# Converting float64 weights: rebias, shift, sign and an integer add, 512 columns a piece, and second weights used in place

## The chip, the cores and the metric

The kernel runs on one core of one Trainium2 chip. The time is device microseconds (us) of one execution of the whole program. The engines are TensorE (PE, matrix products; its weight loads are listed apart as PEld), VectorE (DVE), ScalarE (ACT), GpSimd (POOL) and SyncE (SP), which here only issues DMAs. Each engine works through its own instructions in program order; semaphores make it wait for others.

## The reference

The program is an attention followed by a mixing block with a two-layer perceptron, over 8 batches of 576 tokens, 8 heads of 64:

```python
def _attn_ref(q, k, v, s):
    scores = scale * np.matmul(q, k.transpose(0, 1, 3, 2))
    cum = np.cumsum(np.maximum(s, 0.0), axis=-1)
    bias = -(cum[:, :, :, None] - cum[:, :, None, :])
    scores = np.where(causal, -1000000000.0, scores + np.minimum(bias, 0.0))
    ...
    return np.matmul(attn, v)

def _moe_ref(x, w_ch1, w_ch2):
    X = np.fft.fft(np.fft.fft(x, axis=1), axis=2)
    u = x + np.real(X)
    un = (u - mu) / np.sqrt(var + 1e-06)
    ch = np.maximum(un @ w_ch1, 0.0) @ w_ch2
    return u + ch
```

The two weight matrices (512 x 2048 and 2048 x 512) arrive as 64-bit numbers: the host takes numpy's float64 arrays as pairs of 32-bit words and does no arithmetic on them. The kernel makes 32-bit floats of them, 2 million numbers in all. A double's high word has the sign, 11 bits of exponent and the upper 20 bits of the mantissa; the low word has the other 32. A float has 8 bits of exponent and 23 of mantissa.

## The kernel before

**Stages.** The batches' heads are worked off as 32 pairs (stage one, some 545 us): scores, exponentials, products with the values, and the Fourier products of earlier batches woven in. Then comes a transition, in which the attention ends, the last Fourier products run, and the perceptron begins on the first two tiles of 512 tokens. Seven more tiles follow in `fast_tile`.

**Weights.** The 2048 hidden units are 16 groups `f` of 128. For each f, `wP[f]` holds 128 partitions x 1024 numbers: 512 of the first matrix, 512 of the second. The kernel keeps each converted number as a high part (rounded to the matmul's 32-bit format) and a low rest, so that three products give nearly full precision: `wh`, `wl` for the first matrix, `w2h`, `w2l` for the second. The first weights stay in SBUF; the second ones are kept in DRAM (`w2D`) and read again for each tile.

**Conversion.** A piece is WC = 256 columns. Its raw words are loaded (`raw`, 8 bytes a number). `hi` is the high word, `lo` the upper 16 bits of the low word; both are read with a step of 8 bytes. DVE isolates the exponent bits (L85 or L1110); ACT rebiases and scales them (Relu with a bias, L86 or L1112); DVE makes an integer of the mantissa bits (L87 or L1115), adds `lo` scaled by 2^-16 (L90 or L1117), puts the sign onto the exponent's power of two (L89 or L1120); POOL multiplies the two (L91 or L1123).

- For f = 0 to 5 (`NC` = 6) this is done during the attention by `convert_w` (L95), a generator that is woven between the other streams of a pair; its tiles are in the pool `attb`, and the floats go to DRAM (`wD`).
- For f = 6 to 15 (`N1` = 6) it is done in the transition by `piece` (L1099). `late_first` (L1186) makes the first weights, two pieces for each f, split on ACT and DVE by `split_w` (L1127); those of f = 6 and 7 in the pool `stage2`, those of f = 8 to 15 in the pool `stage3`, which opens when the Fourier tables' space is released. `late_second` (L1175) makes the second weights, two pieces for each f, split on ACT and POOL into the buffers `cvh` and `cvl` (two of each); `keep_second` (L1138) stores both to `w2D`.

**Order of the transition.** It is not written out by hand: a small planner (`Flow`, L1613) simulates the engines at build time. Each generator yields steps (engine, cost, what it depends on, a ring of buffers with so many readers) and emits its instruction when the planner picks it: of the steps that can start first on an engine, the one with the earliest due time. Costs come from `act`, `dve`, `dvp`, `pool_` and `dma` (L1678 to L1695). The order in which steps are picked is the order of the instructions on each engine and of the DMAs on SP.

**Steps of the perceptron there.** `todo` (L1310) lists 32 steps n in four parts p: tile one with f = 0 to 5 (p = 0), tile two with f = 0 to 5 (p = 1), tile one with f = 6 to 15 (p = 2, n = 12 to 21), tile two with f = 6 to 15 (p = 3). A step is a first product (L1433: 24 matmuls with `wh`, `wl`), the rectified result split by ACT and DVE (L1299, L1301), and a second product (L1413 to L1415), which PE runs behind the first product of step n + 1. For p > 0, `second_loads` (L1315) reads a step's second weights from `w2D` into one of four slots of the ring `w2`, as soon as the step four before has been multiplied:

```python
            _, hold = yield wait(ev("w2taken"), ring=(ring("w2", 4), 1))
            t = second()
            got = Last(ev("S", n), 2)
            for x in range(2):
                e = yield dma(256, ev("w2D", f))
                nc.sync.dma_start(out=t[x].bitcast(F32), in_=w2D[x, f])
                got.add(e)
            S2[n] = (*t, hold)
```

After the last second weights are stored, `sums_flow` (L1460) forms the sums of first weights that the fast tiles need (`sums_w`, L113).

Of the kernel before, what the change touches and what calls it, by code (L numbers as in the profile page):

```python
# [42 lines left out]
def fused_kernel(ctx, tc, qkT, vA, sP, wP, tabD, tabS, corr, out):  # L43
# [21 lines left out]
    nc.vector.memset(eps, 1e-6)  # L65
    wbias = const.tile([128, 1], F32, name="wbias")
    nc.vector.memset(wbias, -8.0 * WEXP)


# [3 lines left out]

    WC = 256

    def rounded(pool, f, x, bufs):

        m = pool.tile([128, WC], I32, tag="wm", name="wm", bufs=bufs)
        raw = pool.tile([128, 2 * WC], I32, tag="raw", name="raw", bufs=bufs)
        nc.sync.dma_start(out=raw, in_=wP[f, :, WC * x:WC * x + WC].bitcast(I32))  # L80
        hi = raw.rearrange("p (n w) -> p n w", w=2)[:, :, 1]
        lo = raw.bitcast(U16).rearrange("p (n w) -> p n w", w=4)[:, :, 1]
        yield 0.0
        e = pool.tile([128, WC], I32, tag="we", name="we", bufs=bufs)
        nc.vector.tensor_scalar(e, hi, 0x7FF00000, None, op0=ALU.bitwise_and)  # L85
        nc.scalar.activation(e, e, AF.Relu, bias=wbias, scale=8.0)  # L86
        nc.vector.tensor_scalar(m, hi, 0xFFFFF, 0x100000, op0=ALU.bitwise_and, op1=ALU.bitwise_or)  # L87
        yield 0.4
        nc.vector.scalar_tensor_tensor(out=e, in0=hi, scalar=-0x80000000, in1=e, op0=ALU.bitwise_and, op1=ALU.bitwise_or)  # L89
        nc.vector.scalar_tensor_tensor(out=m.bitcast(F32), in0=lo, scalar=2.0 ** -16, in1=m, op0=ALU.mult, op1=ALU.add)  # L90
        nc.gpsimd.tensor_mul(e.bitcast(F32), m.bitcast(F32), e.bitcast(F32))  # L91
        yield 0.4
        return e.bitcast(F32)

    def convert_w(pool, lo, hi, bufs):  # L95

        for f in range(lo, hi):
            for x in range(1024 // WC):
                m = yield from rounded(pool, f, x, bufs)
                nc.sync.dma_start(out=wD[f, :, WC * x:WC * x + WC], in_=m)  # L100
                yield 0.2
# [442 lines left out]
    for M in Ms:  # L544
        nc.vector.memset(M, 0.0)
    amask = att.tile([128, 640], BF16, name="amask")
    nc.gpsimd.memset(amask, 0.0)
    nc.gpsimd.affine_select(out=amask[:, 512:640], in_=amask[:, 512:640], pattern=[[-1, 128]], compare_op=ALU.is_ge, fill=NEG, base=0, channel_multiplier=1)
    trash = att.tile([128, 512], BF16, name="trash")
# [48 lines left out]
    def maxes(i):  # L598
        st = sts[i]
        qy, ky = st["qy"], st["ky"]  # L600
        M = Ms[i % 2]
        M1 = att.tile([128, 4], F32, tag="M1", name="M1", bufs=2)
        for h in range(2):
            for c in range(5):
                nk = 128 * c + 128 if c < 4 else S
                parts = [(0, max(nk, 256))] if c < 4 else [(0, 256), (256, 320)]
                col = M[:, 5 * h + c:5 * h + c + 1]
                for x, (k0, n) in enumerate(parts):
                    p = psm.tile([128, 512], F32, tag="m", name="pm", bufs=5)
                    nc.tensor.matmul(p[:, :n], qy[:, h, 128 * c:128 * c + 128], ky[:, h, k0:k0 + n], start=True, stop=True)  # L610
                    if len(parts) > 1 and not x:
                        first = M1[:, h:h + 1]
                        nc.vector.tensor_reduce(out=first, in_=p[:, :n], axis=AX.X, op=ALU.max)
                    else:
                        n = nk - k0
                        m0 = 512 - 128 * c + k0
                        nc.vector.tensor_tensor_reduce(out=trash[:, :n], in0=p[:, :n], in1=amask[:, m0:m0 + n], scale=1.0,  # L617
                                                       scalar=first if x else NEG, op0=ALU.add, op1=ALU.max, accum_out=col)
# [3 lines left out]
        nc.tensor.transpose(out=p[0:10, 0:128], in_=M, identity=ident)  # L622
# [103 lines left out]
    mixing = None  # L726
    weights = convert_w(attb, 0, NC, 2)
    tiles = list(range(0, NT, TOK))
# [370 lines left out]
    def piece(where, f, x, bufs, then):  # L1099


        e, rhold = yield dma(256, ring=(ring(where + "raw", bufs), 2))
        home = stages[where]
        raw = home.tile([128, 2 * WC], I32, tag="raw", name="raw", bufs=bufs)
        nc.sync.dma_start(out=raw, in_=wP[f, :, WC * x:WC * x + WC].bitcast(I32))
        hi = raw.rearrange("p (n w) -> p n w", w=2)[:, :, 1]
        lo = raw.bitcast(U16).rearrange("p (n w) -> p n w", w=4)[:, :, 1]
        e1, hold = yield ("DVE", 0.42, (e,), (ring(where + "we", bufs), 1))
        n = home.tile([128, WC], I32, tag="we", name="we", bufs=bufs)
        nc.vector.tensor_scalar(n, hi, 0x7FF00000, None, op0=ALU.bitwise_and)  # L1110
        e1 = yield act(400, e1)
        nc.scalar.activation(n, n, AF.Relu, bias=wbias, scale=8.0)  # L1112
        _, mhold = yield ("DVE", 0.42, (e,), (ring(where + "wm", bufs), 1))
        m = home.tile([128, WC], I32, tag="wm", name="wm", bufs=bufs)
        nc.vector.tensor_scalar(m, hi, 0xFFFFF, 0x100000, op0=ALU.bitwise_and, op1=ALU.bitwise_or)  # L1115
        e = yield dve(256)
        nc.vector.scalar_tensor_tensor(out=m.bitcast(F32), in0=lo, scalar=2.0 ** -16, in1=m, op0=ALU.mult, op1=ALU.add)  # L1117
        rhold.add(e)
        e = yield dve(256, e1)
        nc.vector.scalar_tensor_tensor(out=n, in0=hi, scalar=-0x80000000, in1=n, op0=ALU.bitwise_and, op1=ALU.bitwise_or)  # L1120
        rhold.add(e)
        e = yield pool_(256, e)
        nc.gpsimd.tensor_mul(n.bitcast(F32), m.bitcast(F32), n.bitcast(F32))  # L1123
        mhold.add(e)
        yield from then(n.bitcast(F32), e, hold)

# [20 lines left out]
    def load_w(f, home):  # L1147
# [14 lines left out]
        W2now[f] = (vh, vl, hold)  # L1162
        flow.add(keep_second(f, (vh, vl), hold), due_w(f) + 20.0)

# [9 lines left out]

    def late_second():  # L1175


        for f in range(N1, NF):
            _, hold = yield wait(ring=(ring("cv", 2), 2))
            t = [stages["stage2"].tile([128, 512], F32R, tag=f"cv{y}", name=f"cv{y}", bufs=2) for y in "hl"]  # L1180
            ready = Last(ev("W2", f), 2)
            flow.add(keep_second(f, t, hold), late_due(f) - 20.0)
            for x in (2, 3):
                flow.add(piece("stage2", f, x, 4, split_w(*t, slice(WC * x - 512, WC * x - 256), WC, True, ready)), late_due(f) - 30.0 + x)

    def late_first(home, where, bufs, f0, f1):  # L1186
        for f in range(f0, f1):
            wh = home.tile([128, 512], F32R, tag=f"wh{f}", name=f"wh{f}")
            wl = home.tile([128, 512], F32R, tag=f"wl{f}", name=f"wl{f}")
            W[f] = (wh, wl)  # L1190
            ready = Last(ev("W", f), 2)
            for x in (0, 1):
                flow.add(piece(where, f, x, bufs, split_w(wh, wl, slice(WC * x, WC * x + WC), WC, False, ready)), late_due(f) - 20.0 + x)

# [272 lines left out]
    def tail():  # L1467
# [222 lines left out]
def pool_(n, *deps, ring=None):  # L1690
    return "POOL", 0.15 + n * 0.0024, deps, ring

# [157 lines left out]
```

## Time and profile before

| | us |
|---|---|
| three runs | 1436.44, 1430.39, 1432.87 |
| median | 1432.87 |
| the profiled execution, its own time | 1428.06 |
| its span, first to last instruction | 1426.3 |
| stage 0 to 545 (attention) | 545 |
| stage 545 to 814 (transition) | 269 |
| stage 814 to 1426 (fast tiles) | 612 |

The mean granted clock of TensorE in that execution is 0.967 of full speed. In the profile, L12 is line 12 of the kernel's source; `out<-in` names the tiles written and read; a group's row gives the count, the busy time in us and the mean duration in ns, and then how long the engine had stood idle before these instructions and for whom. In a row by tile, the three durations are the smallest, the median and the largest in ns. Matmuls are pipelined, so a busy PE isn't PE at its peak.

### The profile page before, as it was taken

How to read it: one execution, taken by the hardware profiler on the slowest of the kernel's cores; microseconds unless marked ns; L12 is line 12 of the kernel's file. 1: busy time of each engine (PE TensorE's matmuls, PEld its weight loads, DVE VectorE, ACT ScalarE, POOL GpSimd, SP SyncE). 2: the span in 40 equal slices, each digit the busy share in tenths (PEclk: the TensorE clock that was granted, in tenths of full speed). 3: DMA queues.
4: the chain of work that ended last, by engine and by line, in shares of the span. 5: the costliest groups of instructions: out<-in, count | busy, mean ns of one | idle time of the engine just before them, and what ended most of it. 6: DMA issues, size and time to landing. Idle time of an engine off the chain costs nothing.

```text
span 1426.3 us, 21949 instructions
## 1 busy us (share of the span) xinstructions
PE 1285.1 (90%) x7582; PEld 1122.4 (79%) x7582; DVE 878.1 (62%) x1989; ACT 627.8 (44%) x1472; POOL 522.1 (37%) x541
## 2 busy tenths in 40 slices
PE   4886979797979898889879989999999999999998
PEld 3665867686867677779768878888888888898987
DVE  6667686768685756798984477544445453544423
ACT  4664757474756565543432333333333333333221
POOL 6444565556564646545562243110201111021100
PEclk9999999898999999999979999999999999999999
DMA  8565555464655545648644332534434343343333
GB/s 198 155 186 157 144 163 159 149 168 152 170 161 145 153 117 162 211 152 279 226 162 158 111 118 89 170 126 142 144 121 161 103 159 129 128 157 104 134 119 118
DMA packets 128907, 216.06 MB, mean 151 GB/s; under 512 B 16826, under 2 KB 41850, under 8 KB 128796
## 3 DMA queue, kind: packets, MB, share of 16 engines
q1 hardware_dynamic: 126795, 211.60, 48.5%
q0 software_dynamic: 1712, 2.53, 0.9%
q8 instruction: 60, 0.98, 0.3%
q10 hardware_dynamic: 288, 0.52, 0.1%
q14 instruction: 52, 0.42, 0.1%
HBM read 158.93 MB, written 31.72 MB: 134 GB/s over the span
## 4 chain that ended last, share of the span: by engine, by line
PE 48%; DVE 8%; POOL 2%; issue 1%; ACT 1%; DMA 1%; SPq 0%; POOLq 0%; DVEq 0%; ACTq 0%
PE b L331 19%; PE acc L242 7%; PE acc L243 7%; PE acc L244 7%; PE h L1433 3%; PE acc L1415 1%; PE acc L1414 1%; PE acc L1413 1%; DVE wm L1117 1%; DVE we L1120 1%; DVE we L1110 1%; DVE wm L1115 1%; DVE wl L1132 1%; PE pz L1005 1%; DVE zl L1301 1%
## 5 line engine op out<-in xcount | busy, mean ns | idle before, releaser
L610 PE MATMUL pm<-KQ 128*128 128x256 f32 (+3 forms) x384 | 157.7, 430 | 46.4 <-DVE Mx L617 26.7
L646 ACT ACTIVATE P<-ps 128x256 f32<-128x256 f32 x372 | 141.7, 393 | 121.6 <-PE ps L643 117.6
L674 PE MATMUL pavB<-P,va 128*128 128x320 f32 x600 | 180.8, 394 | 9.4 <-ACT stage L678 9.4
L242 PE MATMUL acc<-zh,w2h 128*128 128x512 f32 x452 | 179.0, 396 | 0.0
L243 PE MATMUL acc<-zh,w2l 128*128 128x512 f32 x452 | 179.0, 396 | 0.0
L244 PE MATMUL acc<-zl,w2h 128*128 128x512 f32 x452 | 178.4, 395 | 0.0
L289 POOL TENSOR_TENSOR w<-w,o 128x512 f32<-128x512 f32 x28 | 37.9, 1364 | 353.4 <-DVE o L285 312.8
L642 PE MATMUL ps<-KQ 128*128 128x256 f32 x372 | 148.7, 403 | 14.6 <-ACT P L646 5.8
L617 DVE CUSTOM_DVE_ANT_0 trash<-pm,amask 128x128 bf16<-128x128 f32 (+3 forms) x256 | 123.6, 483 | 42.8 <-PE pm L610 25.8
L610 PEld LDWEIGHTS pm<-KQ 128*128 128x128 f32 x384 | 78.9, 209 | 69.5 <-DVE Mx L617 36.9
L323 ACT ACTIVATE zh<-cs 128x256 fp32r<-128x256 f32 x112 | 58.8, 525 | 143.6 <-DVE cs L343 89.1
L643 PE MATMUL ps<-Q,K 128*128 128x256 f32 x372 | 117.1, 318 | 2.1 <-POOL Q L590 2.1
L674 PEld LDWEIGHTS pavB<-P,va 128*128 128x128 f32 x600 | 102.0, 199 | 16.7 <-ACT stage L678 13.3
L590 POOL TENSOR_TENSOR Q<-qk,Q 64x576 fp32r<-64x576 f32 x64 | 99.4, 1567 | 40.2 <-DMA Q<-KQ 28.5
L324 DVE SCALAR_TENSOR_TENSOR zl<-cs,zh 128x256 fp32r<-128x256 f32 x112 | 65.9, 588 | 69.2 <-ACT zh L323 69.2
L587 DVE TENSOR_TENSOR K<-qk,KQ 64x576 fp32r<-64x576 f32 x64 | 61.3, 957 | 73.1 <-ACT KQ L573 54.0
L642 PEld LDWEIGHTS ps<-KQ 128*128 128x128 f32 x372 | 74.6, 201 | 37.6 <-ACT P L646 11.1
L331 PEld LDWEIGHTS b<-bh,wh 128*128 128x128 f32 x448 | 84.1, 189 | 24.5 <-DVE cs L343 5.2
L244 PEld LDWEIGHTS acc<-zl,w2h 128*128 128x128 f32 x452 | 85.3, 189 | 20.4 <-DVE zl L324 0.4
L331 PE MATMUL b<-bh,wh 128*128 128x256 f32 x448 | 89.6, 281 | 3.9 <-DVE cs L343 3.9
L331 PE MATMUL b<-bh,wl 128*128 128x256 f32 x448 | 90.2, 283 | 0.0
L331 PE MATMUL b<-bl,wh 128*128 128x256 f32 x448 | 89.6, 281 | 0.0
(271 smaller groups left out, 3163.9 us busy)
## 6 DMA issues: line engine op xcount, KB each, us to landing
w2h<-w2D SPq DMA_DIRECT2D x138, 256.0 KB
w2l<-w2D SPq DMA_DIRECT2D x138, 256.0 KB
qk<-in_qkT_dram SPq DMA_DIRECT2D x32, 576.0 KB
raw<-in_wP_dram SPq DMA_DIRECT2D x64, 256.0 KB
va<-in_vA_dram SPq DMA_DIRECT2D x32, 480.0 KB
u<-uD SPq DMA_DIRECT2D x10, 1024.0 KB
Q<-KQ SPq DMA_DIRECT2D x32, 288.0 KB
K<-KQ SPq DMA_DIRECT2D x32, 288.0 KB
```

The source lines that it names most:

```text
L242: nc.tensor.matmul(acc[j], a[:, cs], y, start=first, stop=False)
L243: nc.tensor.matmul(acc[j], b[:, cs], y, start=False, stop=False)
L244: nc.tensor.matmul(acc[j], a[:, cs], z, start=False, stop=final)
L324: nc.vector.scalar_tensor_tensor(out=y[1][:, at], in0=src, scalar=0.0, in1=y[0][:, at].bitcast(F32), op0=ALU.max, op1=ALU.subtract)
L331: nc.tensor.matmul(p[:, 0:256], a[:, j * 128:(j + 1) * 128], b[:, j], start=start and i == 0, stop=i == 5, skip_group_check=not start)
L590: nc.gpsimd.tensor_sub(q1[64:128, h], qk[0:64, h], q1[0:64, h].bitcast(F32))
L610: nc.tensor.matmul(p[:, :n], qy[:, h, 128 * c:128 * c + 128], ky[:, h, k0:k0 + n], start=True, stop=True)
L617: nc.vector.tensor_tensor_reduce(out=trash[:, :n], in0=p[:, :n], in1=amask[:, m0:m0 + n], scale=1.0, scalar=first if x else NEG, op0=ALU.a ...
L642: nc.tensor.matmul(p[:nk, :n], ky[:, h, ksl], qy[:, h, a:a + n], start=True, stop=False)
L643: nc.tensor.matmul(p[:nk, :n], k1[:, h, ksl], q1[:, h, a:a + n], start=False, stop=True)
L646: nc.scalar.activation(P[:nk, o:o + a + n - lo], p[:nk, lo - a:n], AF.Exp, scale=0.125)
L674: nc.tensor.matmul(p[:, a - lo:n], va[:nk, c, vs], P[:nk, o:o + w], start=c == 0, stop=c == cs[-1])
```

## The change

- A piece is 512 columns in place of 256.
- The conversion goes another way. ACT multiplies the high word, read as a float, by 2^-112 (`rebias`): the sum of the exponent's upper bits and the bias comes out right, while the bits stand three places too low. DVE shifts left by three (`shift`) and sets the sign bit (`sign`). ACT scales the 16 bits of `lo` by 2^-13 and rounds to an integer (`rest`), which is written over the low word in the raw tile. POOL adds the two as 32-bit integers (`carry`).
- In the attention the conversion's tiles move from the pool `attb` to `atop`; `amask` shrinks from 640 to 512 columns. The steps of a piece are further apart in the woven order (a yield behind each).
- In the transition `late_second` is gone. For p = 2 `second_loads` converts a step's second weights straight into its slot of the ring `w2` (three readers: PE and two stores), and `keep_second` stores them from there for p = 3 and the later tiles. `late_first` has one piece for each f. The rings of raw and converted pieces have 3 buffers each, in place of 4 and 6.
- The planner's costs of ACT, DVE and POOL instructions are raised.

```diff
+    def rebias(y, hi):
+        nc.scalar.activation(y.bitcast(F32), hi.bitcast(F32), AF.Copy, scale=2.0 ** -112)
+    def shift(y):
+        nc.vector.tensor_scalar(y, y, 3, None, op0=ALU.logical_shift_left)
+    def sign(y, hi):
+        nc.vector.scalar_tensor_tensor(out=y, in0=hi, scalar=-0x80000000, in1=y, op0=ALU.bitwise_and, op1=ALU.bitwise_or)
+    def rest(r, lo):
+        nc.scalar.activation(r, lo, AF.Relu, scale=2.0 ** -13)
+    def carry(y, r):
+        nc.gpsimd.tensor_tensor(out=y, in0=y, in1=r, op=ALU.add)
...
-    weights = convert_w(attb, 0, NC, 2)
+    weights = convert_w(atop, 0, NC, 2)
...
-        e1, hold = yield ("DVE", 0.42, (e,), (ring(where + "we", bufs), 1))
-        n = home.tile([128, WC], I32, tag="we", name="we", bufs=bufs)
-        nc.vector.tensor_scalar(n, hi, 0x7FF00000, None, op0=ALU.bitwise_and)
-        e1 = yield act(400, e1)
-        nc.scalar.activation(n, n, AF.Relu, bias=wbias, scale=8.0)
-        _, mhold = yield ("DVE", 0.42, (e,), (ring(where + "wm", bufs), 1))
...
-        nc.gpsimd.tensor_mul(n.bitcast(F32), m.bitcast(F32), n.bitcast(F32))
+        e1, hold = yield ("ACT", 0.6, (e,), (ring(where + "we", bufs), 1))
+        y = home.tile([128, WC], I32, tag="we", name="we", bufs=bufs)
+        rebias(y, a)
+        e1 = yield ("DVE", 0.45, (e1,), None)
+        shift(y)
+        e1 = yield dve(512, e1)
+        sign(y, a)
+        rhold.add(e1)
+        e = yield act(512, e)
+        rest(r, b)
+        e = yield pool_(512, e, e1)
+        carry(y, r)
...
-            _, hold = yield wait(ev("w2taken"), ring=(ring("w2", 4), 1))
+            _, hold = yield wait(ev("w2taken"), ring=(ring("w2", 4), 3 if p == 2 else 1))
             t = second()
+            if p == 2:
+                S2[n] = (*t, hold)
+                yield wait(ev("staged"))
+                flow.add(piece("stage2", f, 1, 3, split_w(*t, slice(0, WC), WC, True, Last(ev("S", n), 1))), mlp_due(n) - 14.0)
+                flow.add(keep_second(f, t, hold, ev("S", n)), mlp_due(n) + 8.0)
+                continue
...
-        late_first(w1, "stage2", 4, N1, NW)
-        flow.add(late_second(), 55.0)
+        late_first(w1, "stage2", 3, N1, NW)
+        ev("staged").set(ev("out", L))
...
-    return "ACT", 0.03 + n * 0.00095, deps, ring
+    return "ACT", 0.16 + n * 0.0009, deps, ring
...
-    return "DVE", 0.1 + n * 0.0014, deps, ring
+    return "DVE", 0.18 + n * 0.0014, deps, ring
...
-    return "DVE", 0.08 + n * 0.00105, deps, ring
+    return "DVE", 0.12 + n * 0.0011, deps, ring
...
-    return "POOL", 0.15 + n * 0.0024, deps, ring
+    return "POOL", 0.2 + n * 0.0024, deps, ring
```

More of the change, by code (lines that the diff above doesn't have):

```diff
@@ L72, in split, with words @@
         nc.vector.tensor_sub(dst_l, src, dst_h.bitcast(F32))
[L74 to L93, printed above, removed]
+    WC = 512
+    def words(raw):
+        both = raw.rearrange("p (n w) -> p n w", w=2)
+        return both[:, :, 1], both[:, :, 0], raw.bitcast(U16).rearrange("p (n w) -> p n w", w=4)[:, :, 1]
+    def rebias(y, hi):
[8 more added lines that the diff above has]
+        nc.gpsimd.tensor_tensor(out=y, in0=y, in1=r, op=ALU.add)
     def convert_w(pool, lo, hi, bufs):
@@ L98, in convert_w @@
             for x in range(1024 // WC):
-                m = yield from rounded(pool, f, x, bufs)
-                nc.sync.dma_start(out=wD[f, :, WC * x:WC * x + WC], in_=m)
+                raw = pool.tile([128, 2 * WC], I32, tag="raw", name="raw", bufs=bufs)
+                nc.sync.dma_start(out=raw, in_=wP[f, :, WC * x:WC * x + WC].bitcast(I32))
+                a, r, b = words(raw)
+                yield 0.0
+                y = pool.tile([128, WC], I32, tag="we", name="we", bufs=bufs)
+                rebias(y, a)
+                yield 0.4
+                shift(y)
+                yield 0.4
+                sign(y, a)
+                yield 0.4
+                rest(r, b)
+                yield 0.4
+                carry(y, r)
+                yield 0.2
+                nc.sync.dma_start(out=wD[f, :, WC * x:WC * x + WC], in_=y.bitcast(F32))
                 yield 0.2
@@ L1099, in piece @@
     def piece(where, f, x, bufs, then):
-        e, rhold = yield dma(256, ring=(ring(where + "raw", bufs), 2))
+        e, rhold = yield dma(512, ring=(ring(where + "raw", bufs), 2))
         home = stages[where]
@@ L1105, in piece @@
         nc.sync.dma_start(out=raw, in_=wP[f, :, WC * x:WC * x + WC].bitcast(I32))
-        hi = raw.rearrange("p (n w) -> p n w", w=2)[:, :, 1]
-        lo = raw.bitcast(U16).rearrange("p (n w) -> p n w", w=4)[:, :, 1]
-        e1, hold = yield ("DVE", 0.42, (e,), (ring(where + "we", bufs), 1))
-        n = home.tile([128, WC], I32, tag="we", name="we", bufs=bufs)
-        nc.vector.tensor_scalar(n, hi, 0x7FF00000, None, op0=ALU.bitwise_and)
-        e1 = yield act(400, e1)
-        nc.scalar.activation(n, n, AF.Relu, bias=wbias, scale=8.0)
-        _, mhold = yield ("DVE", 0.42, (e,), (ring(where + "wm", bufs), 1))
[L1114 to L1117, printed above, removed]
-        rhold.add(e)
[L1119 to L1125, printed above, removed]
+        a, r, b = words(raw)
+        e1, hold = yield ("ACT", 0.6, (e,), (ring(where + "we", bufs), 1))
+        y = home.tile([128, WC], I32, tag="we", name="we", bufs=bufs)
+        rebias(y, a)
+        e1 = yield ("DVE", 0.45, (e1,), None)
+        shift(y)
+        e1 = yield dve(512, e1)
+        sign(y, a)
+        rhold.add(e1)
+        e = yield act(512, e)
+        rest(r, b)
+        e = yield pool_(512, e, e1)
+        carry(y, r)
+        rhold.add(e)
+        yield from then(y.bitcast(F32), e, hold)
     def split_w(h, low, xs, n, pooled, ready):
@@ L1162, in load_w @@
         W2now[f] = (vh, vl, hold)
-        flow.add(keep_second(f, (vh, vl), hold), due_w(f) + 20.0)
+        flow.add(keep_second(f, (vh, vl), hold, ev("W2", f)), due_w(f) + 20.0)
     W2now = {}
@@ L1173, in late_due @@
         return C0 + 5.6 * (f - N1)
[L1175 to L1184, printed above, removed]
     def late_first(home, where, bufs, f0, f1):
@@ L1190, in late_first @@
             W[f] = (wh, wl)
-            ready = Last(ev("W", f), 2)
-            for x in (0, 1):
-                flow.add(piece(where, f, x, bufs, split_w(wh, wl, slice(WC * x, WC * x + WC), WC, False, ready)), late_due(f) - 20.0 + x)
+            flow.add(piece(where, f, 0, bufs, split_w(wh, wl, slice(0, WC), WC, False, Last(ev("W", f), 1))), late_due(f) - 20.0)
     def norm_flow(t0, free=None):
```

15 lines of the change are left out of this document (6 added, 9 removed).

## The prediction

> **What bounds the kernel now.** I read the busy table first, then the busy time by stage, then the steps of TensorE (PE) in the stage where it is least busy, the waits there, and last the instructions of the weight conversion.
>
> ```profile
> PE 1285.1 (90%) x7582; PEld 1122.4 (79%) x7582; DVE 878.1 (62%) x1989; ACT 627.8 (44%) x1472; POOL 522.1 (37%) x541
> ```
>
> PE is busy for 90% of the span, but that mean hides stages. Cut by stage (columns: PE, weight load, DVE, ACT, POOL busy, granted clock, DMA share, GB/s):
>
> ```profile
> 0.00:545.00 545.00, 448.61 (x2445) 374.44 (x2445) 381.09 (x1116) 330.40 (x810) 296.33 (x328) 0.95 0.58 158
> ...
> 634.00:673.80 39.80, 39.80 (x264) 36.40 (x263) 34.05 (x78) 14.72 (x34) 23.03 (x28) 1.00 0.79 262
> 673.80:756.00 82.20, 65.23 (x361) 57.70 (x360) 74.48 (x146) 30.10 (x67) 47.94 (x55) 0.88 0.59 194
> 756.00:814.00 58.00, 57.47 (x367) 51.87 (x366) 26.31 (x35) 14.62 (x25) 13.65 (x11) 1.00 0.43 139
> 814.00:1426.00 612.00, 601.15 (x3733) 537.92 (x3731) 296.98 (x522) 193.24 (x438) 95.92 (x80) 1.00 0.40 131
> ```
>
> The last 612 us are PE throughout, and no weight is converted there. The hole is 673.8 to 756: PE busy for 65 of 82 us at a granted clock of 0.88, DVE for 74. These are the ten steps of the first tile over f = 6 to 15, each with freshly converted weights.
>
> ```profile
> 673.79 0.64 PE L1433 MATMUL h<-bh,wh 128*128 128x256 f32 x4
> ...
> 756.02 0.28 PE L1433 MATMUL h<-bh,wh 128*128 128x256 f32 x1
> ...
> 761.63 0.28 PE L1433 MATMUL h<-bh,wh 128*128 128x256 f32 x1
> ```
>
> The step that begins at 756.02 takes 5.61 us. Ten such are 56.1; the ten from 673.79 to 756.02 took 82.2. So **26.1 us** are lost in idling and in the slow clock behind it. The waits of PE from 696 to 756 (us in total, times, longest) name the cause:
>
> ```profile
> PE h L1433 <- ACT wh L1130: 8.6, 4, 4.3
> PE h L1433 <- DVE wl L1132: 5.3, 2, 3.1
> ```
>
> Late first weights. Why late, when DVE's instructions are short? Here are two engines at one moment:
>
> ```profile
> 653.97 1.03 POOL L1132 TENSOR_TENSOR cvl<-we,cvh 128x256 fp32r<-128x256 f32 x1 [0.52 <-ACT cvh L1130]
> ...
> 654.32 0.83 DVE L1110 TENSOR_SCALAR we<-raw 128x256 int32<-128x256 int32 x1
> ```
>
> DVE's 0.83 ends at 655.15, just after POOL's instruction ends at 655.00. Alone the same DVE form takes 0.29 (below). So a DVE instruction that works on SBUF waits inside itself for POOL, and the two engines' SBUF work is nearly serial. Its sum comes from the rows of the converted tile (ns min/median/max), with the rows of the other POOL work between 630 and 742 (the adds L1068, then L1361, then L1352):
>
> ```profile
> L1110 DVE TENSOR_SCALAR we<-raw x40: 278/290/1384, 624.6 to 738.1; 128x256 int32<-128x256 int32 x40
> L1112 ACT ACTIVATE we<-we,wbias x40: 493/510/514, 625.2 to 738.4; 128x256 int32<-128x256 int32 x40
> L1120 DVE SCALAR_TENSOR_TENSOR we<-raw,we x40: 409/418/1025, 631.1 to 739.8; 128x256 int32<-128x256 int32 x40
> L1123 POOL TENSOR_TENSOR we<-wm,we x40: 722/742/1127, 631.6 to 740.9; 128x256 f32<-128x256 f32 x40
> ...
> L1132 POOL TENSOR_TENSOR cvl<-we,cvh x20: 731/892/1028, 634.1 to 742.2; 128x256 fp32r<-128x256 f32 x20
> ...
> L1132 DVE TENSOR_TENSOR wl<-we,wh x20: 405/418/983, 647.1 to 741.0; 128x256 fp32r<-128x256 f32 x20
> ...
> 630.00:742.00 112.00, 6.87 (x8) 0.92 0.65 215
> 630.00:742.00 112.00, 5.49 (x4) 0.92 0.65 215
> 630.00:742.00 112.00, 5.24 (x4) 0.92 0.65 215
> ```
>
> Successive DVE instructions overlap by about 0.08 us, so I take 0.21 for a 0.29 and 0.34 for a 0.42. L1115 and L1117 have the same two shapes. POOL: 40 x 0.74 + 20 x 0.73 + 17.6 = 61.8. DVE: 40 x (0.21 + 0.21 + 0.34 + 0.34) + 20 x 0.34 = 50.8. Together 112.6, in a stretch of 112. **The serial DVE and POOL work fills the conversion's time completely; that is the bound of this stage.**
>
> **The change, part by part.** The terms at 512 columns need these rows:
>
> ```profile
> L1132 POOL TENSOR_TENSOR w2l<-w2l,w2h x6: 1263/1295/1667, 579.2 to 617.3; 128x512 fp32r<-128x512 f32 x6
> L1301 DVE SCALAR_TENSOR_TENSOR zl<-h,zh 128x512 fp32r<-128x512 f32 x32 | 21.8, 681 | 24.6 <-ACT zh L1299 24.5
> L1130 ACT CAST cvh<-we x20: 388/406/409, 633.6 to 741.7; 128x256 fp32r<-128x256 f32 x20
> L1130 ACT CAST w2h<-w2l 128x512 fp32r<-128x512 f32 x6 | 3.7, 619 | 0.0
> ```
>
> *Conversion.* A 512-column piece had eight DVE instructions, two ACT and two POOL; it gets two DVE (shift, sign), two ACT and one POOL. The sign has L1120's form: 0.42 at 256 becomes 0.68 at 512 (L1301), 0.60 start to start. The shift has L1110's form: 0.13 shorter than the other at 256, so half its slope, 0.42 at 512 and 0.34 start to start. With the other's full slope it is 0.55 and 20 shifts cost 2.6 us more; no row excludes that. ACT: L1112 at 0.51 plus the slope of a cast (0.62 - 0.41) is 0.72 for the rest, 0.62 for the rebias: 20 x 1.34 = 26.8 against 40 x 0.51 = 20.4; ACT has 52 us free between 673.8 and 756, so I cost it at nothing. The POOL add replaces two multiplies. No row has an integer add or operands 8 bytes apart on POOL; its floor is 1.26, a plain 512-column row, its ceiling I set at twice that row, 2.6. I take 1.30, as the nearest row.
>
> *Splits.* The first weights' subtraction on DVE goes from two 0.34 to one 0.60; the second weights' on POOL from two 0.73 to one 1.30.
>
> One f (a first and a second piece) then costs 2 x (0.34 + 0.60) + 0.60 + 3 x 1.30 = 6.38; it was (50.8 + 44.2) / 10 = 9.5. Ten: 63.8, with the other 17.6, 81.4 against 112.6: 31 us less serial work, more than the 26.1 lost.
>
> *Second weights in place.* They were converted from 631 on (L1120's first) into buffers cvh and cvl, stored, and read back for steps from 679 on. Now their piece starts only when one of the four w2 slots is free, that is, when PE is four steps behind it; and the first weights of f = 8 to 15 start, as before, once the Fourier tables' space is released. That is after the last row of u leaves:
>
> ```profile
> 658.78 0.27 SPq L1096 DMA_DIRECT2D uD<-rows  x1
> ```
>
> So the reserve that was worked off from 630 to 658 is gone, and after 658.8 there remain 8 first pieces (0.94 + 0.60 + 1.30 = 2.84) and 10 second ones (0.94 + 2.60 = 3.54): 22.7 + 35.4, plus L1361 and L1352, 10.7: 68.8. 658.8 + 68.8 = **727.6**. PE at full rate wants the last first weights at 673.8 + 9 x 5.61 = 724.3 and the last second ones at 732.8. It fits, at 93% use. Two engines with chained instructions don't reach that without gaps; I let 6 of the 26.1 us stay, and take **-20**. The bounds: -26 (nothing lost) and 0.
>
> The added wait: each store of a second half waits on SP for its split, with the next raw loads queued behind; the stores stood there before too. Removed: 20 reads of 256 KB in these steps, while DMA in the stage is at 0.59; I count nothing. What is late next: the sums of the first four first weights (L123 to L143) begin when the last second half is stored, and keep their place relative to PE.
>
> *Attention.* The same conversion for f = 0 to 5 lies beside 31 head pairs:
>
> ```profile
> L85 DVE TENSOR_SCALAR we<-raw 128x256 int32<-128x256 int32 x24 | 11.0, 458 | 0.2
> L89 DVE SCALAR_TENSOR_TENSOR we<-raw,we 128x256 int32<-128x256 int32 x24 | 10.3, 431 | 1.1 <-ACT we L86 1.1
> L90 DVE SCALAR_TENSOR_TENSOR wm<-raw,wm 128x256 f32<-128x256 uint16 x24 | 10.1, 421 | 0.5
> ...
> L87 DVE TENSOR_SCALAR wm<-raw 128x256 int32<-128x256 int32 x24 | 9.5, 395 | 0.0
> ...
> PE pm L610 <- DVE Mx L617: 21.5, 16, 4.4
> PE pmt L622 <- DVE Mx L617: 19.4, 14, 3.4
> ```
>
> DVE falls from 40.9 to 12 x 1.10, stretched as now by 1.2, 15.9: 25 us, 6.6% of its 381. If PE's 40.9 us behind DVE shrink in proportion, that is **-3**. ACT gains 12 x 1.34 - 24 x 0.51 = 3.9; all of it on the path would give +4; the other end is -10, a quarter of the 40.9.
>
> *Planner's costs.* act, dve, dvp and pool_ become dearer, which reorders the whole planned stage from 546 on.
>
> ```profile
> 546.00:577.00 31.00, 22.99 (x131) 18.90 (x129) 18.49 (x31) 19.18 (x48) 16.02 (x17) 1.00 0.44 151
> 577.00:617.70 40.70, 38.01 (x232) 34.80 (x232) 31.31 (x43) 18.46 (x35) 24.74 (x21) 0.92 0.72 237
> 617.70:634.00 16.30, 10.85 (x56) 9.52 (x55) 14.40 (x25) 6.11 (x15) 3.52 (x3) 0.79 0.17 59
> ```
>
> PE idles 8.0 + 2.7 + 5.5 = 16 us before 634; nothing in the profile prices another order. I take 0, between -5 and +5.
>
> **Sum:** -20 - 3 + 0 = **-23**. Against the profiled execution's own 1428.06 us (span 1426.3) that is 1405; that execution lies below the three runs, whose median is 1432.87, so on their scale **1410**.
>
> One page speaks against it. The Trainium skill, GPSIMD Engine Reference, Performance pitfalls for Q7 kernels, says that reads whose step exceeds 8 bytes cost some 2.9 cycles an element in place of 1.9; the rounded rest lies exactly 8 bytes apart, at that edge, and no run here shows which side it is on. By the rule as written the add stays at 1.30; on its far side my estimate from that page would be 1.95, and the sum -11.
>
> **Rivals.** *A, the add is long.* At its ceiling of 2.6, 18 adds bring 18 x 1.3 = 23 us back: 658.8 + 92 = 751, nearly the old end. -3 and -3 of attention: 1427. For it: no row prices this add. Against: L1123 and L1132 on POOL cost the same, whichever operation.
>
> *B, slower: the second weights come late in place.* A slot is free at the end of step n-4's second product, and needed some 3.5 steps later, 19.6 us at full rate. One load's row in the chain of waits, and the loads' row:
>
> ```profile
> 606.06 2.26 DMA raw<-in_wP_dram
> ...
> L1105 SPq DMA_DIRECT2D raw<-in_wP_dram x40: 327/402/1811, 606.1 to 720.0; - x40
> ```
>
> Alone the chain is short: twice 2.26 for 512 KB, then 0.62 + 0.42 + 0.68 + 1.30 + 0.62 + 1.30, 9.5. In the full queues it was longer: the last load went out at 720.0, the last POOL subtraction ended at 742.9: 23 us. The steps took 8.22 now, so the rival decides once slot to ready exceeds 3.5 x 8.22 = 29 us. At 33 a step takes 9.4 and ten lose 12: 1442. Against it: the queues hold 28% less work.
>
> *C, attention gains its whole 10 and nothing stalls later:* -26 - 10, 1397.
>
> **How the numbers follow.** Forecast, 1400 to 1421: 0.68. A, 1422 to 1435: 0.17. B, 1440 and above: 0.08. C, below 1400: 0.07. The range 1396 to 1429 takes in the forecast, most of C and the larger half of A. About 0.5%, 7 us, is what a measurement here can tell from no change: faster holds the forecast, C and 0.07 of A, 0.82; same 0.10; slower 0.08.
>
> **What would show it.** Right: from 673.8 on ten steps in 56 to 65 us, PE's waits for ACT wh and DVE wl under 5 us, DVE far from full, adds near 1.3, shifts near 0.42. A: adds over 2 us, DVE's shift and sign stretched behind them. B: PE waiting at L1413 for w2h or w2l where it waited at L1433. The attention term is wrong if the stage before 545 moves by over 10 us, and the whole if an order made by the new costs opens a new hole before 634.

## The result and the profile after

The changed kernel takes **1411.70 us** (median of four runs, 1406.97 to 1416.26), the kernel before 1432.16 (1430.39 to 1436.44): a ratio of **0.985, interval 0.981 to 0.990**. With four more runs of it, taken later, the median of eight is 1408.4. Faster by 1.5%, then, and 1.7 us from the 1410 that was predicted. The sum came out right; of its three terms only the largest has the right size, as the experiments show.

The profiled execution took 1416.26 us, its span is 1414.6. The busy table and the busy time by stage, cut at the same marks as before (end of attention; n = 0; n = 12; n = 22; first fast tile; end):

```profile
PE 1280.3 (91%) x7582; PEld 1117.6 (79%) x7582; DVE 817.8 (58%) x1786; ACT 634.4 (45%) x1452; POOL 517.0 (37%) x499
```

```profile
0.00:565.00 565.00, 459.66 (x2445) 383.63 (x2446) 366.03 (x1047) 336.52 (x813) 298.51 (x317) 0.92 0.56 153
565.00:594.00 29.00, 23.08 (x136) 19.61 (x135) 15.33 (x28) 19.58 (x50) 13.00 (x16) 1.00 0.53 177
594.00:685.40 91.40, 86.59 (x549) 78.14 (x549) 66.26 (x99) 39.56 (x75) 45.23 (x37) 0.94 0.59 196
685.40:745.30 59.90, 56.27 (x361) 50.51 (x360) 44.24 (x47) 28.12 (x50) 46.59 (x35) 1.00 0.66 220
745.30:809.00 63.70, 60.21 (x366) 53.77 (x365) 31.20 (x45) 17.46 (x30) 17.39 (x16) 0.95 0.38 126
809.00:1414.00 605.00, 594.52 (x3733) 531.90 (x3731) 294.76 (x522) 193.19 (x438) 96.26 (x80) 1.00 0.40 132
```

Of the kernel before, the one stage that the prediction doesn't show at these marks (n = 0 to n = 12):

```profile
577.30:673.80 96.50, 88.64 (x547) 80.69 (x548) 79.54 (x143) 39.30 (x82) 50.99 (x51) 0.93 0.65 218
```

Three things are to be seen. The ten steps from n = 12 to 22 went from 82.2 to 59.9 us, and the granted clock there from 0.88 to 1.00: the hole is gone from these steps. The attention, which the change was not to lengthen, ends at 565 in place of 545. And the fast tiles, whose instructions are the same, took 605 in place of 612. The ten steps by their first products, and all that PE waited for between 630 and 746:

```profile
685.43 0.64 PE L1432 MATMUL h<-bh,wh 128*128 128x256 f32 x4
...
745.30 0.64 PE L1432 MATMUL h<-bh,wh 128*128 128x256 f32 x4
```

```profile
PE acc L1412 <- DVE o L1344: 3.3, 1, 3.3
PE acc L1414 <- DVE zl L1294: 0.3, 1, 0.3
```

The 8.6 and 5.3 us behind wh and wl (L1433 before, L1432 now) are gone. What is left is a wait for `o`, the DVE instruction that reads a finished sum `acc` and so frees it for PE: in DVE's order it stands behind shifts and signs of the conversion.

Not all of the gain is kept, though. From the first product of n = 22 to that of n = 31, the last step of the transition, the kernel before took 52.2 us, this execution 58.0 and the second trace of the changed kernel 53.2. PE's two longest waits there, from 743 to 812:

```profile
PE acc L1414 <- DVE zl L1294: 1.7, 1, 1.7
PE acc L1412 <- ACT zh L1292: 1.1, 1, 1.1
```

The zh that PE waits for stands on ACT behind the sums of first weights (L143, L152), and from 751.0 to 756.4 the granted clock is 0.50. The kernel before had the same two waits (1.1 and 1.8) one step earlier, at n = 21, inside the ten steps. So the mark at n = 22 flatters the change: from n = 12 to n = 31 it is 134.5 us before, 117.9 and 114.8 after, a gain of 17 to 20 us.

The late conversion's own instructions (ns min/median/max):

```profile
L77 ACT ACTIVATE we<-raw x20: 652/660/687, 635.0 to 736.9; 128x512 f32<-128x512 f32 x20
L80 DVE TENSOR_SCALAR we<-we x20: 409/870/1568, 635.7 to 737.7; 128x512 int32<-128x512 int32 x20
L83 DVE SCALAR_TENSOR_TENSOR we<-raw,we x20: 675/694/1687, 636.4 to 738.7; 128x512 int32<-128x512 int32 x20
L89 POOL TENSOR_TENSOR we<-we,raw x20: 1302/1366/1782, 639.1 to 739.5; 128x512 int32<-128x512 int32 x20
...
L1138 DVE TENSOR_TENSOR wl<-we,wh x10: 674/988/1856, 643.0 to 718.9; 128x512 fp32r<-128x512 f32 x10
...
L1138 POOL TENSOR_TENSOR w2l<-we,w2h x10: 1291/1302/1487, 684.8 to 741.6; 128x512 fp32r<-128x512 f32 x10
```

The smallest values are the prices: shift 0.41 (0.42 predicted), sign 0.68 (0.68), add 1.30 (1.30). The distance between smallest and largest is DVE blocked while POOL works: the same shift takes 0.41 or 1.57, and the difference, 1.16, is nearly a whole add. One case, from the timelines of both engines:

```profile
687.26 1.37 POOL L89 TENSOR_TENSOR we<-we,raw 128x512 int32<-128x512 int32 x1 [1.14 <-DVE we L83]
```

```profile
687.50 1.68 DVE L83 SCALAR_TENSOR_TENSOR we<-raw,we 128x512 int32<-128x512 int32 x1
```

POOL's add ends at 688.63 and DVE's sign at 689.18, 0.55 us later. The subtraction zl, which reads h from PSUM, is not held: its 32 instructions took 0.63 to 0.69 us.

### The profile page after: what moved, and what is told of

The parts are those of the page before. It is cut to its first block, busy times and chain, and to the rows that moved or that the text cites. A ratio compares the mean times of both kernels' runs of the same rounds, so it can differ in the third digit from the quotient of the medians.

```text
span 1414.6 us, 21592 instructions
## 1 busy us (share of the span) xinstructions
PE 1280.3 (91%) x7582; PEld 1117.6 (79%) x7582; DVE 817.8 (58%) x1786; ACT 634.4 (45%) x1452; POOL 517.0 (37%) x499
## 4 chain that ended last, share of the span: by engine, by line
PE 50%; DVE 5%; POOL 3%; ACT 3%; issue 2%; DMA 2%; SPq 0%; POOLq 0%; ACTq 0%; DVEq 0%
PE b L342 19%; PE acc L254 7%; PE acc L253 7%; PE acc L255 7%; PE h L1432 3%; PE acc L1414 1%; PE acc L1413 1%; PE acc L1412 1%; POOL we L89 1%; PE pav L877 1%; PE pavB L685 1%; DVE we L83 1%; DVE we L80 1%; DMA raw<-in_wP_dram 1%; PE pz L1016 0%
## 5 line engine op out<-in xcount | busy, mean ns | idle before, releaser
L621 PE MATMUL pm<-KQ 128*128 128x256 f32 (+3 forms) x384 | 161.5, 439 | 46.8 <-DVE Mx L628 28.0
L685 PE MATMUL pavB<-P,va 128*128 128x320 f32 x600 | 184.4, 401 | 1.3 <-ACT stage L689 1.2
L598 DVE TENSOR_TENSOR K<-qk,KQ 64x576 fp32r<-64x576 f32 x64 | 61.4, 960 | 90.6 <-ACT KQ L584 82.3
L685 PEld LDWEIGHTS pavB<-P,va 128*128 128x128 f32 x600 | 105.3, 204 | 6.3 <-ACT stage L689 2.7
L660 POOL TENSOR_SCALAR_AFFINE_SELECT P<-P 128x512 f32<-128x512 f32 x62 | 44.2, 713 | 133.4 <-ACT P L657 130.8
```

Of the source, the lines that this page charges most:

```text
L685: nc.tensor.matmul(p[:, a - lo:n], va[:nk, c, vs], P[:nk, o:o + w], start=c == 0, stop=c == cs[-1])
```

## The experiments

Twelve kernels were run, in three groups of four, each group with its own runs of the kernel before. The first group asks which part of the change did what.

**The changed kernel again** (no edit).

> The changed kernel once more, for a second trace of it. In the first trace its attention ends 17 to 20 us later than in the kernel before, and its seven fast tiles, whose instructions are the same, take 6.7 us less. If both belong to the kernel, they show again: first h product of n = 0 near 594, fast tiles 84.3 us each, time 1412. If they are variation between executions, n = 0 moves by over 5 us towards 577, or a fast tile goes towards 85.2.

Measured: 1406.21 us (1403.81 to 1414.06), n = 0 at 591.8, fast tiles 84.3. Both belong to the kernel.

**Old attention, new transition.**

The old `rounded` (256 columns), the old `convert_w` and wbias are back for f = 0 to 5.

```diff
-    weights = convert_w(atop, 0, NC, 2)
+    weights = convert_w(attb, 0, NC, 2)
...
-    amask = att.tile([128, 512], BF16, name="amask")
+    amask = att.tile([128, 640], BF16, name="amask")
```

> The changed kernel with the old conversion in the attention (256 columns a piece, five DVE instructions, pool attb, the old spacing of its steps); the transition keeps the new one. Theory T1, the new conversion makes the attention longer: n = 0 begins near 577 in place of 594, ten steps stay near 60, time 1396 to 1401. Theory T2, the longer attention is variation of one execution: time within 4 us of the changed kernel, 1408 to 1416. My prediction's attention term (-3) taken at its word: 3 us slower than the changed kernel, 1415.

Measured: 1411.49 us (1404.86 to 1415.11), n = 0 at 585.6, ten steps 59.4, fast tiles 85.2. By its time alone this is theory T2. But n = 0 comes 6 to 9 us earlier, and the fast tiles are at their old length: two effects may cancel here. That led to the second group.

**New attention, old transition** (the reverse edit, on the kernel before; wbias stays).

> The kernel before with only the attention's conversion new; the transition keeps the old conversion, its buffers and the old costs. T1: n = 0 near 590 to 594, ten steps still 82, time 1440 to 1449. T2: 1428 to 1436, as before. The prediction's term: 1430.

Measured: 1440.51 us (ten runs, 1434.39 to 1445.68), ratio 1.006 (1.005 to 1.008); ten steps 83.5; n = 0 at 581.3, short of the 590 to 594 of theory T1. The new conversion in the attention, as the change issues it, **costs** 9 us.

**Only the planner's costs** (on the kernel before).

```diff
-    return "ACT", 0.03 + n * 0.00095, deps, ring
+    return "ACT", 0.16 + n * 0.0009, deps, ring
...
-    return "POOL", 0.15 + n * 0.0024, deps, ring
+    return "POOL", 0.2 + n * 0.0024, deps, ring
```

> The kernel before with only the planner's four raised costs. The prediction's term is 0, between -5 and +5: 1428 to 1438, the ten steps near 82. If the costs make a better order by themselves, the ten steps fall below 76 and the time below 1425, and part of what I put down to shorter DVE and POOL work belongs to them.

Measured: 1424.22 us (ten runs), ratio 0.996 (0.993 to 0.998): 7.5 us faster. n = 0 to 12 takes 91.9 in place of 96.5, the ten steps 79.0 in place of 82.2, so neither of the two expectations (82, or under 76) holds for them.

The second group follows the fast tiles. With wbias dropped, the tiles in the pools behind it lie 32 bytes lower in SBUF: in the built programs `bh`, the first product's moving operand, begins at byte 25792 of its partition before and 25760 after (403 and 402.5 times 64). Not every tile moves. The pools that are allocated from the other end keep these places, among them `wB` with the first weights of f = 8 to 15.

**The changed kernel with a spare constant.**

```diff
+    spare = const.tile([128, 1], F32, name="spare")
+    nc.vector.memset(spare, 0.0)
```

> The changed kernel with one unused constant of four bytes a partition in place of the dropped wbias, so that every later tile lies 32 bytes higher in SBUF, where the kernel before has it. Theory P, the place of the tiles sets the rate of the matmuls: the fast tiles go back from 84.3 to 85.2 us each (6.7 us in all); if nothing else depends on the place, 1413 to 1416. If the attention depends on it too, the other way round (its end at 553 in the run with the new attention alone, 560 and 565 in the changed kernel), n = 0 begins near 582 to 586 and the time is 1403 to 1409. Theory N, the place does nothing: 84.3 us a tile, 1406 to 1411.

**The kernel before, two constants in one tile.**

```diff
-    eps = const.tile([128, 1], F32, name="eps")
+    both = const.tile([128, 2], F32, name="eps")
+    eps, wbias = both[:, 0:1], both[:, 1:2]
     nc.vector.memset(eps, 1e-6)
-    wbias = const.tile([128, 1], F32, name="wbias")
```

> The kernel before with eps and wbias as two columns of one tile, so that every later tile lies 32 bytes lower, where the changed kernel has it; nothing else differs. P: fast tiles 84.3 us in place of 85.2, time 1424 to 1427, if the attention keeps its length; 1428 to 1434 if the attention loses there what the fast tiles gain. N: 85.2 and 1432.

The reciprocal that DVE makes once in each fast tile is a clock for it. In the timelines of DVE of four kernels, the second and the last one shown are four tiles apart; first the kernel before, then the changed one, then the one before with two constants in one tile, then the changed one with the spare constant:

```profile
957.77 3.34 DVE L196 RECIPROCAL r<-r 128x512 f32<-128x512 f32 x1
...
1298.62 3.34 DVE L196 RECIPROCAL r<-r 128x512 f32<-128x512 f32 x1
```

```profile
951.06 3.34 DVE L207 RECIPROCAL r<-r 128x512 f32<-128x512 f32 x1
...
1288.28 3.34 DVE L207 RECIPROCAL r<-r 128x512 f32<-128x512 f32 x1
```

```profile
963.13 3.34 DVE L196 RECIPROCAL r<-r 128x512 f32<-128x512 f32 x1
...
1300.36 3.34 DVE L196 RECIPROCAL r<-r 128x512 f32<-128x512 f32 x1
```

```profile
949.07 3.34 DVE L209 RECIPROCAL r<-r 128x512 f32<-128x512 f32 x1
...
1289.92 3.34 DVE L209 RECIPROCAL r<-r 128x512 f32<-128x512 f32 x1
```

Four tiles take 340.85 and 337.22 us, and with the places exchanged 337.23 and 340.85. The times follow: 1424.36 us for the kernel before with the places moved (ratio 0.996, 0.994 to 0.998), 7.4 faster; 1413.75 for the changed kernel with the old places, 5.3 slower than the 1408.4. Theory P holds, both ways. It is not the attention: that ended at 563 and 547, as in the kernels without the edit. The steps of the transition narrow it down. Where PE doesn't wait, steps on f = 0 to 7, whose first weights move along with bh, take 5.61 to 5.63 us at either place. Steps on f = 8 to 15, whose first weights stay, take 5.60 to 5.63 with the old places and 5.57 or 5.58 with the new ones; in the kernel before with moved places the change falls between n = 13 (f = 7, 5.62) and n = 14 (f = 8, 5.57). So the traces point to the place of bh against that of the first weights. Why 32 bytes matter there isn't settled.

**The changed kernel with the old costs.**

> The changed kernel with the planner's four old costs. If the raised costs are worth here what they were worth in the kernel before (7.5 us), 1414 to 1419, with the ten steps of n = 12 to 21 at 64 to 70 us. If they only mended what the long old conversion had spoilt, 1405 to 1411 and ten steps near 60. The prediction's term for them is 0.

Measured: 1415.62 us (1413.17 to 1417.12), 7 us slower than the 1408.4. The ten steps stay at 61.4. What is lost lies on both sides of them: n = 0 to 12 takes 96.0 in place of 91 to 92, and n = 22 to 31 takes 59.7 in place of 53.2 to 58.0. The costs are worth 7 us here too, but neither theory placed them right.

**Old attention, new transition, moved places.**

> Old conversion in the attention, new transition, and eps and wbias in one tile (tiles where the changed kernel has them). If the new attention costs 9 us wherever the tiles lie, and the place gives the fast tiles 6.7: 1397 to 1403, the best so far. If the place costs the attention as much as it gives: 1408 to 1413, fast tiles at 84.3 and n = 0 later than 585.6.

Measured: 1401.91 us (1397.37 to 1403.79), ratio 0.978 (0.975 to 0.981); n = 0 at 581.9, fast tiles 84.3. Faster than the changed kernel by 6.5: again the new attention's price, with bh at the same place.

The third group asks why.

**A piece of the attention's conversion in two groups.**

```diff
                 rebias(y, a)
-                yield 0.4
+                rest(r, b)
                 shift(y)
-                yield 0.4
+                yield 0.8
                 sign(y, a)
-                yield 0.4
-                rest(r, b)
-                yield 0.4
                 carry(y, r)
+                yield 0.8
                 yield 0.2
```

> The changed kernel with a piece of the attention's conversion issued in two groups, as the old conversion was (rebias, rest and shift together, then sign and add), in place of five steps apart. Theory O, order: the new attention is long because its steps, spread out, change the order on SP; in five pairs the store of the finished rows (xs from xr), which waits for POOL, stands ahead of the load of the next q and k, and in none of the kernel before. In this kernel's order it stands ahead in none. Then pair 10 ends near 177 in place of 188, the attention (last mt) at 545 to 550 in place of 560 to 565, time 1396 to 1403. Theory I, the longer instructions themselves hold up exponentials and loads: pair 10 still near 188, 1405 to 1412.

Measured: **1388.13 us** (1379.92 to 1392.69), ratio **0.970 (0.968 to 0.973)**: 20 us faster than the changed kernel and 14 faster than the old attention with moved places. The attention ends at 526. The instructions are the same, the tiles' places are the same and PE's order, which is fixed by hand, is the same; only the order on the other engines and on SP differs. So the order is worth the 20 us, and theory I falls. Theory O forecast less (545 to 550, and 1396 to 1403 us), so what it names is at most a part. Pair 10 shows that part. SP's timeline of the changed kernel, the maxima's store (KQ from mt) of the pair before first and of this pair last:

```profile
165.60 0.84 SPq L636 DMA_DIRECT2D KQ<-mt  x1
169.19 0.58 SPq L694 DMA_DIRECT2D sums<-rows  x1
173.90 0.54 SPq L723 DMA_DIRECT2D xs<-xr  x1
...
176.69 0.64 SPq L569 DMA_DIRECT2D qk<-in_qkT_dram  x1
...
188.70 0.82 SPq L636 DMA_DIRECT2D KQ<-mt  x1
```

POOL's timeline at that point, and the waits of ACT and of PE from 165 to 189:

```profile
172.45 1.43 POOL L721 TENSOR_TENSOR xr<-stage,rb 128x576 f32<-128x576 f32 x1
```

```profile
ACT KQ L584 <- DMA qk<-in_qkT_dram: 6.0, 1, 6.0
```

```profile
PE ps L653 <- ACT P L657: 5.3, 1, 5.3
```

SP stands from 169.8 to 173.9 before the store of xr, which POOL finishes at 173.88. Behind it stands the load of q and k for a later pair, so it goes out at 176.69. ACT comes to the copy of that q and k, waits 6.0 us, and the exponentials behind it in ACT's queue are late for PE by 5.3. No conversion instruction is in this chain. SP's timeline of the grouped kernel for the same pair:

```profile
159.81 0.84 SPq L634 DMA_DIRECT2D KQ<-mt  x1
...
164.06 0.58 SPq L567 DMA_DIRECT2D qk<-in_qkT_dram  x1
169.93 0.56 SPq L721 DMA_DIRECT2D xs<-xr  x1
...
176.63 0.83 SPq L634 DMA_DIRECT2D KQ<-mt  x1
```

The load goes first, 5.87 us ahead of the store, and the pair takes 16.8 us in place of 23.1. That explains one pair out of several. By the copies of mt in the two traces, pairs 19, 29 and 31 are 7, 5 and 8 us shorter too, and pair 20 is 7 longer. Of the five pairs with the store ahead of the load, 10 and 19 lose by it; 6, 11 and 26 come out within 1.5 us of the grouped kernel's. So what holds up most of the pairs stays open.

**Not in place.** `late_second` is back, with one 512-column piece for each f into cvh and cvl.

```diff
-            _, hold = yield wait(ev("w2taken"), ring=(ring("w2", 4), 3 if p == 2 else 1))
+            _, hold = yield wait(ev("w2taken"), ring=(ring("w2", 4), 1))
...
-        ev("staged").set(ev("out", L))
+        flow.add(late_second(), 55.0)
```

> The changed kernel with second weights of f = 6 to 15 converted as before the change into the two cv buffers, from 630 on, stored and read back for p = 2; arithmetic, 512 columns and raised costs stay. The prediction counted nothing for working in place: 1404 to 1414, ten steps 58 to 64. If working in place is what helps (no round trip by way of DRAM, one transfer less on SP): ten steps over 66, 1416 to 1424. If it hurts, because a reserve worked off early would do better: ten steps at 56 to 57, 1402 to 1406.

Measured: 1418.86 us (1414.25 to 1426.43), 10 slower than the 1408.4; ten steps 73.8. PE's waits from 686 to 770, and SP's from 720 to 762:

```profile
PE acc L1414 <- ACT zh L1300: 8.8, 1, 8.8
PE acc L1414 <- DMA w2h<-w2D: 3.2, 1, 3.2
PE acc L1415 <- DMA w2l<-w2D: 0.9, 1, 0.9
```

```profile
SPq L1327 <- PE acc L1416: 12.7, 1, 12.7
SPq L1147 <- ACT cvh L1136: 11.8, 3, 4.7
```

SP waits 11.8 us to store halves that are still being converted, with the reads of other halves queued behind, and PE waits 4.1 us for reads. The larger wait, 8.8, is for the zh of n = 21, in front of which the sums of first weights stand on ACT. So working in place is worth 10 us here, but only the 4.1 are seen to come from the round trip through DRAM; whether the round trip also brings about the planner's order on ACT isn't shown. With the sums counted in both kernels, n = 12 to 31 takes 126.1 us against 114.8 to 117.9.

**A second add on POOL** (of the same operands, into a spare tile, for each late piece).

```diff
+        spare = home.tile([128, WC], I32, tag="spare", name="spare", bufs=1)
...
+        nc.gpsimd.tensor_tensor(out=spare, in0=y, in1=r, op=ALU.add)
         carry(y, r)
```

> The changed kernel with one more integer add on POOL, of the same operands into a spare tile, ahead of each of the 20 late pieces' adds; the planner isn't told. It stands for rival A, an add of 2.6. Theory S, DVE and POOL are in effect one engine here and 93% used: 18 of the adds after 658.8 bring 23 us, ten steps take 76 to 84 and the time is 1424 to 1432. Theory F, POOL has room of its own: ten steps 60 to 66, 1406 to 1414.

Measured: 1433.25 us (ten runs, 1427.25 to 1440.23), 25 slower than the 1408.4, for 20 adds of 1.3 = 26 us, and inside the 1422 to 1435 of rival A, for whose long add this stands. Ten steps 77.2. The window of the ten steps, the rows of the converted tile, and PE's waits from 677 to 758:

```profile
679.07:756.23 77.16, 61.90 (x361) 52.99 (x360) 48.52 (x48) 30.26 (x54) 67.69 (x48) 0.89 0.53 171
```

```profile
L80 DVE TENSOR_SCALAR we<-we x20: 410/960/1557, 627.9 to 751.5; 128x512 int32<-128x512 int32 x20
L83 DVE SCALAR_TENSOR_TENSOR we<-raw,we x20: 674/1651/1744, 628.6 to 752.5; 128x512 int32<-128x512 int32 x20
L1130 POOL TENSOR_TENSOR spare<-we,raw x20: 1290/1318/1764, 631.3 to 753.3; 128x512 int32<-128x512 int32 x20
L89 POOL TENSOR_TENSOR we<-we,raw x20: 1287/1572/1642, 633.2 to 754.7; 128x512 int32<-128x512 int32 x20
```

```profile
PE acc L1414 <- DVE o L1346: 8.3, 2, 5.2
PE acc L1416 <- DVE zl L1296: 4.8, 4, 2.9
PE acc L1414 <- ACT zh L1294: 1.9, 1, 1.9
```

POOL is busy for 67.7 of 77.2 us. DVE's sign, which is not touched, goes from 0.69 to 1.65 in the median. The hole is back with its clock, 0.89. PE waits for no weight there. Of its 15.0 us of waits 13.1 are for o and zl, and 11.2 of these come before 721, with o and zl in DVE's order behind instructions that POOL holds. Theory F falls, and the numbers of theory S come out: work of one engine is paid by both. But not all of the 25 us need go by way of DVE. From 736 on DVE idles 3.5 to 4.5 us at a time, waiting for ACT's rebias, which stands behind a cast that waits for POOL's add: there POOL's own queue is full.

**Grouped attention, low part of late second weights on DVE.**

```diff
-                flow.add(piece("stage2", f, 1, 3, split_w(*t, slice(0, WC), WC, True, Last(ev("S", n), 1))), mlp_due(n) - 14.0)
+                flow.add(piece("stage2", f, 1, 3, split_w(*t, slice(0, WC), WC, False, Last(ev("S", n), 1))), mlp_due(n) - 14.0)
```

> The kernel with the grouped attention, and the late second weights' low part subtracted on DVE (0.6 to 0.7 us) in place of POOL (1.3 us). By theory S the serial work falls by 10 x 0.65 = 6.5 us, and what the ten steps still lose to late weights (59.9 against 56.1) goes: 0 to 4 us faster than the grouped kernel. By theory F DVE, which has the sums of zh's rest and the next tile's sums to do as well, becomes the later one: 0 to 5 us slower.

Measured: 1386.61 us (1379.61 to 1390.74), ratio 0.968 (0.964 to 0.971), against 0.970 (0.968 to 0.973) of the grouped kernel: no difference that these runs can tell, and the expected 0 to 4 us aren't excluded either. Ten steps 59.8 against 61.5. PE's only wait in them is for DVE's o, 2.2 us against 2.6, so little was left to win there.

All kernels in one table, from the starts in their timelines (attention: last copy of mt; then n = 0; then the two stretches; one fast tile from the reciprocals):

| kernel | time | attention | n = 0 | n 0 to 12 | n 12 to 22 | fast tile |
|---|---|---|---|---|---|---|
| before | 1432.2 | 545.3 | 577.3 | 96.5 | 82.2 | 85.2 |
| changed | 1411.7 | 565.5 | 594.4 | 91.0 | 59.9 | 84.3 |
| changed, again | 1406.2 | 560.3 | 591.8 | 92.1 | 61.6 | 84.3 |
| old attention | 1411.5 | 550.4 | 585.6 | 92.1 | 59.4 | 85.2 |
| new attention alone | 1440.5 | 553.0 | 581.3 | 97.7 | 83.5 | 85.2 |
| new costs alone | 1424.2 | 545.6 | 578.4 | 91.9 | 79.0 | 85.2 |
| changed, spare constant | 1413.8 | 563.1 | 592.2 | 92.7 | 61.1 | 85.2 |
| before, places moved | 1424.4 | 547.2 | 581.3 | 97.4 | 83.4 | 84.3 |
| changed, old costs | 1415.6 | 557.5 | 586.2 | 96.0 | 61.4 | 84.3 |
| old attention, places moved | 1401.9 | 546.9 | 581.9 | 91.9 | 59.4 | 84.3 |
| grouped | 1388.1 | 526.1 | 560.4 | 91.5 | 61.5 | 84.3 |
| not in place | 1418.9 | 565.6 | 594.9 | 91.9 | 73.8 | 84.3 |
| second add | 1433.3 | 556.1 | 585.2 | 93.9 | 77.2 | 84.3 |
| grouped, DVE | 1386.6 | 532.4 | 568.6 | 91.9 | 59.8 | 84.3 |

The places are from one profiled execution each and the times from several. The old instruction order of the attention ended at 545.3, 545.6, 546.9, 547.2 and 550.4, and the order with five steps a piece between 553.0 and 565.6, so differences of 5 and of 12 us there tell nothing by themselves.

## Why the prediction was right in its sum and wrong in its terms

- **Its own tests.** Ten steps in 56 to 65 us (59.9), waits for wh and wl under 5 us (none), adds near 1.3, shifts near 0.42: all came true. So did the one against its attention term, which is wrong if the stage before 545 moves by over 10 us: it moved by 20.
- **The bound, serial DVE and POOL work: right.** In the 112 us DVE was busy, with the time that POOL held it, for 103.6. The second add brought 25 us for 26 us more on POOL, though in its last part POOL alone was full. The prediction's sum of 112.6 us leaves out some 19 us of DVE work in that window that reads PSUM; rightly, as zl's 0.63 to 0.69 us show. What is late when the serial work is too long need not be a weight: with the second add it is o and zl.
- **The prices: right.** Shift 0.41, sign 0.68, add 1.30. The edge that the Trainium skill names (GPSIMD Engine Reference, Performance pitfalls for Q7 kernels) is not crossed by operands exactly 8 bytes apart, as the rule is written: the add takes 1.30 us, like the plain w2l rows. Rival A falls.
- **The transition, -20: the size right, the share of causes wrong.** The ten steps lost 22.4 us, and 3.8 of the 26.1 stayed (6 predicted), 3.3 of it for o and none for a late weight; up to n = 31 the gain is 17 to 20. But the step "Removed: 20 reads of 256 KB in these steps, while DMA in the stage is at 0.59; I count nothing" failed. Without working in place, and with everything else, n = 12 to 31 takes 126.1 us. Less serial work and the costs together bring 8.4 (134.5 to 126.1), the costs alone 3.2; working in place brings the other 8 to 11. I looked at the load of the DMA engines, 0.59, where the order counted: on SP for 4.1 us of PE's waits, on ACT for 8.8. Old arithmetic in place was not run, so how the two parts act without each other stays open.
- **Rival B, slower in place: wrong.** PE never waited for w2h or w2l.
- **The planner's costs, 0 between -5 and +5: off the end.** -7.5 alone (0.2 to 0.7% by the interval, so 3 to 10 us), 7 in the changed kernel, over half of it between n = 0 and 12. The prediction had seen 16 us of idle PE there (546 to 634) and found nothing to price another order with.
- **The attention, -3 between -10 and +4: the sign wrong.** The new attention alone costs 9 us, and 6.5 at the other places. The step that failed is the proportion "If PE's 40.9 us behind DVE shrink in proportion". DVE did lose the work (366.0 us busy to 565 against 381.1 to 545), but the spread-out steps changed the order on the queues; in pair 10 PE came to wait for exponentials, and they for a load. With the steps in two groups the same instructions bring 14 us against the old attention: the proportion was as wrong there, in the other direction. Rows of the window from 30 us to the attention's end, of the old attention at the moved places and of the grouped one:

```profile
30.00:547.00 517.00, 441.33 (x2423) 371.20 (x2423) 357.54 (x1053) 321.22 (x796) 277.70 (x294) 0.93 0.57 156
```

```profile
30.00:526.00 496.00, 428.27 (x2416) 358.99 (x2416) 341.36 (x979) 321.50 (x794) 276.37 (x282) 0.96 0.59 162
```

DVE loses 16.2 us there and the stretch 21, at a better clock (0.96 for 0.93), with ACT and POOL unchanged.

- **Not seen at all: the fast tiles, -5 to -7.** The change drops a constant of four bytes a partition, and tiles behind it move by 32.

In the measured times the parts are: places -5 to -7, costs -7, in place -10, attention +7 to +9. The change as a whole is -23 (1408.4 against 1431.7, the first group's median of before). If the parts add, what is left, about -8, belongs to the shorter conversion of the late weights; no run shows it by itself. So the forecast of -23 met -23 because the late conversion's two parts together (-18) came near the -20, and the costs and the places, each put at nothing, made up for the attention. That last part is luck.

## What to carry to other kernels

When an edit changes how often a generator hands over, compare the order of the instructions on each queue before and after, DMA issues above all: here the same instructions in two groups in place of five steps were worth 20 us, more than the arithmetic that was the point of the change (some 8, by subtraction). Where two engines block each other, price the instructions that block as one engine's work, and show it by adding work to the one that looks idle. When a stage is cut at a mark, look behind the mark for what moved across it. Before crediting a change with a gain in code that it doesn't touch, hold the places of the tiles fixed.

## What the hardware showed

- A DVE instruction that works on SBUF alone can be held until POOL's ends: the shift takes 0.41 us or up to 1.57, the sign 0.68 or up to 1.74. One that reads an operand from PSUM was not held: zl took 0.63 to 0.69.
- The place of tiles in SBUF changes the rate of matmuls: with bh 32 bytes lower and the first weights of f = 8 to 15 where they were, a fast tile takes 84.3 us in place of 85.2, 1.1%, at a granted clock of 1.00 in both the kernel before and the changed one.
- An integer add of 512 columns on POOL, one operand 8 bytes apart, takes 1.30 us, the time of a subtraction of plain floats (1.29).
